# Gate and up projections by seven products of sums of quarters in place of eight, with the sums of the weights formed once

## The chip, the cores and the metric

The kernel runs on one core of one Trainium2 chip. The metric is the device time of one launch in microseconds; the time before is 1982.77 us, the median of 3 runs (1982.16 to 1983.45). All times below that are read from the profile belong to one profiled execution of 1983.66 us, whose span from the first to the last instruction is 1981.9 us.

## The reference

Two layers are applied to x of 2048 tokens by 448 features, each an attention block and then a gated block; the weights are the same in both layers.

```python
def _A_ref(x, wqkv, wo):            # H = 16 heads of 28
    q, k, v = ...                   # x @ wqkv, (1, 16, 2048, 28) each
    scores = jnp.einsum("bhqd,bhkd->bhqk", q, k) * (Dh ** -0.5)
    p = _softmax(scores, axis=-1)
    o = jnp.einsum("bhqk,bhkd->bhqd", p, v)
    return merged(o) @ wo
def _B_ref(x, w_gate, w_up, w_down):
    g = jnp.einsum("bsd,df->bsf", x, w_gate)     # 448 x 1792
    u = jnp.einsum("bsd,df->bsf", x, w_up)       # 448 x 1792
    h = _sigmoid(g) * u
    return jnp.einsum("bsf,fd->bsd", h, w_down)  # 1792 x 448
x = A_x
for _ in range(2):
    x = x + _A_ref(_layernorm(x), A_wqkv, A_wo)
    x = x + _B_ref(_layernorm(x), B_w_gate, B_w_up, B_w_down)
```

All is float32. The kernel gets that accuracy on TensorE by splitting every operand into a high and a low float16 part and adding three products: high by high, high by low, low by high.

## The kernel before

A layer has four stages, one after the other on TensorE: `project` (queries, keys, values), `attend`, `out_project` and `gated`. The order of all work is written out by hand: each engine runs its own instructions in the order of the program, and a semaphore holds an instruction until what it reads is there.

`gated` (L1068) is the stage of the change. Tokens go in four blocks of 512 (`b`), the 1792 hidden features in seven groups of 256 (`p`), so 28 steps in each layer. In a step `by_features_in_fours` (L374) forms four PSUM banks: gate and up for each of two tiles of 128 hidden features, over 512 tokens. The 448 input features are three full slabs of 128 rows and a tail of 64. Each bank takes nine matmuls over the full slabs (L379 to L381), one over the tail with the high part of x in rows 0 to 63 and its low part in rows 64 to 127 (L382, the weights' high part stands in both halves), and one of only 64 rows (L386) for the low part of the tail's weights; these four last ones of 64 rows stand together at the end, two of them in each half of the array's rows. ScalarE then takes the sigmoid (L1125), VectorE multiplies by up (L1126), the product is split in two float16 parts (`split`, L176), and one step later `down` (L1082) adds 24 matmuls of 448 columns (L1089 to L1091) to four PSUM banks that hold the block's output. All split weights of gate and up lie in SBUF during `gated` (`load_gu`, seven tiles of 1 MB).

The next block's x is made ready during the steps, two pieces a step (`Block.steps`, called by `run_fill`): norm, squares (scaling and 32x32 transposes), store and gather through DRAM (which finish the transposition), two empty pieces, and two pieces that split the gathered slabs (`ready`, `part`, L289). For the first block of the stage the same pieces run in `out_project` (L1013), between its 16 token tiles.

The weights are split once, during the attention of layer 0, by `Prepare` (L715): first all tiles are read and measured (for a scale), one every 4 key tiles of attention, then they are read again and split on VectorE (`split`, L804, one every 6 key tiles), and GpSimd's DMA queue carries them to DRAM (`gu_parts`, `write`). A head of attention has 16 key tiles. Two rings of two slots hold the raw tiles and the packed ones.

In `attend` ScalarE takes the exponential of groups of three score tiles (L879). A few tiles are left to VectorE instead (`score_aside`, L881; the table `side`, L850): one in each of heads 0 to 8 of layer 0 and two in each other head. The lines that set it:

```python
        both = 9 if layer == 0 else 0
        for h in range(H):
            for at, kc, qb in ((4, 10, 3), (9, 15, 1)) if h >= both else ((6, 15, 1),):
                side[(h * NT + at) * NB] = (h * NT + kc) * NB + qb
```

SBUF is handed out in slots (`Slots`): 19 of 8 KB per partition (`big`) and 12 of 2 KB (`qrt`), first freed, first used again.

Of the kernel before, what the change touches and what calls it, by code (L numbers as in the profile page):

```python
# [36 lines left out]
XS = 2.0 ** 11  # L37
PS = 2.0 ** -14
# [8 lines left out]
ROUND = 12583039.0  # L47

# [40 lines left out]
def interleaved_layers(ctx: ExitStack, tc: tile.TileContext, x_in, wqkv, wo, w_gate, w_up,  # L89
# [103 lines left out]
    def scaled_low(lo, hi, raw, m):  # L193
        nc.vector.scalar_tensor_tensor(lo, raw, up[:, m:m + 1], hi, op0=ALU.mult,
                                       op1=ALU.subtract)
# [27 lines left out]
    class Block:  # L223


        def __init__(self, b, twice=False):
            self.b = b
            self.twice = twice
# [22 lines left out]
        def parts(self):  # L251
            self.all = big.get("xhl", [P, 8, W], F16)
            self.hi, self.lo = self.all[:, 0:3, :], self.all[:, 3:6, :]
            self.tail = self.all[:, 6, :]
            self.upper = self.all[:, 7, :]
# [26 lines left out]
        def gather(self):  # L282
            rows = self.scr.rearrange("j r i n -> (j r) (i n)")
            self.raw = big.get("xraw", [P, 4, W])
            nc.sync.dma_start(self.raw[:, 0:3, :],
                              rows[0:384].rearrange("(k p) n -> p k n", p=P))
            nc.sync.dma_start(self.raw[0:64, 3, :], rows[384:D])

        def part(self, kt):  # L289
# [7 lines left out]
            else:  # L297
                split_tail(self.tail.rearrange(order, t=TB, i=4), raw)
                if self.twice:
                    nc.scalar.copy(self.upper[64:128].rearrange(order, t=TB, i=4), raw[0:64])  # L300
                big.put(self.raw)

        def steps(self):
            return [self.norm, self.squares,
                    lambda: (self.store((nc.sync, nc.scalar)), self.gather()),
                    lambda: None, lambda: None,
                    lambda: self.ready(0, 1), lambda: self.ready(2, 3)]
# [49 lines left out]
        def drop(self):  # L357
            big.put(self.all)
# [15 lines left out]
    def by_features_in_fours(pms, blk, wh, wl):  # L374


        for o, pm in enumerate(pms):
            for kt in range(3):
                nc.tensor.matmul(pm, wh(o, kt), blk.hi[:, kt, :], start=(kt == 0), stop=False)  # L379
                nc.tensor.matmul(pm, wh(o, kt), blk.lo[:, kt, :], start=False, stop=False)  # L380
                nc.tensor.matmul(pm, wl(o, kt), blk.hi[:, kt, :], start=False, stop=False)  # L381
            nc.tensor.matmul(pm, wh(o, 3), blk.tail, start=False, stop=False)  # L382
        for o, pm in enumerate(pms):
            r = slice(64 * (o % 2), 64 * (o % 2) + 64)
            x = blk.upper if o % 2 else blk.tail
            nc.tensor.matmul(pm, wl(o, 3)[r], x[r], start=False, stop=True,  # L386
                             tile_position=(r.start, 0))
# [16 lines left out]
    gu_parts = dpool.tile([NF // 2, P, 2, 2, 4, 2 * P], F16, name="gu_parts")  # L404
# [310 lines left out]
    class Prepare:  # L715


        def __init__(self):
# [4 lines left out]
            order = [(do, what) for do in (self.measure, self.split) for what in tiles]  # L723
# [3 lines left out]
            for i, (do, what) in enumerate(order):  # L727
# [3 lines left out]
                at += 4 if do == self.measure else 6  # L731
# [14 lines left out]
        def read(self, kind, j):  # L746
# [3 lines left out]
            elif kind == "gu":  # L750
                for i, w in enumerate((w_gate, w_up)):
                    load_rows(self.view(self.next, kind)[:, i], w, j * 2 * P, 2 * P, nc.gpsimd)
            else:
# [8 lines left out]
        def view(self, t, kind):  # L762
            if kind == "gu":
                return t.rearrange("p (w s c) -> p w s c", w=2, s=4)
            return t[:, 0:4 * D].rearrange("p (s n) -> p s n", s=4)

        def step(self, do, what, then):
# [3 lines left out]
            self.write()  # L771
            do(raw, *what)

        def write(self):
            if self.pack:
                nc.gpsimd.dma_start(*self.pack)
                self.pack = None

# [16 lines left out]
        def sizes(self):  # L795
# [5 lines left out]
            nc.vector.tensor_scalar(back[:, 3:4], pw.bitcast(F32)[:, 4:5], 2.0 ** 40, None,  # L801
                                    op0=ALU.mult)

        def split(self, raw, kind, j):  # L804
# [5 lines left out]
            elif kind == "gu":  # L810
                t = big.at(self.packs, "pack", [P, 2, 2, 4, 2 * P], F16)
                for w in range(2):
                    scaled_split(t[:, w, 0], t[:, w, 1], v[:, w], 4 + w, nc.vector)
                self.pack = (gu_parts[j], t)
# [24 lines left out]
    def attend(layer, values, heads, last_values, gate, keep):  # L839
# [11 lines left out]
        both = 9 if layer == 0 else 0  # L851
        for h in range(H):
            for at, kc, qb in ((4, 10, 3), (9, 15, 1)) if h >= both else ((6, 15, 1),):
                side[(h * NT + at) * NB] = (h * NT + kc) * NB + qb
        main = [u for u in range(units) if u not in side.values()]
# [110 lines left out]
        def more(g):  # L966
            if g >= groups:
                return
            for u in main[3 * g:3 * g + 3]:
                if u in side:  # L970
                    begin.append(side[u])
                if u % (NT * NB) == 8:
# [6 lines left out]
                    elif h == H - 1:  # L979
                        gate.load_out()  # L980
                        gate.load_gu()
# [8 lines left out]
        few = both * NT * NB  # L990
        turn = main.index(few) / 3
        paces = (few + both) / max(turn, 1), (quarters + len(side) - few - both) / (groups - turn)
        for g in range(2, groups + 3):
            more(g)
            x = g - 2.25
            due = int(min(x, turn) * paces[0] + max(x - turn, 0) * paces[1])
# [16 lines left out]
    def out_project(outs, gate):  # L1013
# [15 lines left out]

        gate.load_dn()  # L1030
        gate.load_gu()
# [18 lines left out]
    class WeightsGated:  # L1050
        def __init__(self):
            self.gu, self.dn = [], []
# [5 lines left out]
        def load_gu(self):  # L1058
            self.gu.append(big.get("gu", [P, 2, 2, 4, 2 * P], F16))
            nc.sync.dma_start(self.gu[-1], gu_parts[len(self.gu) - 1])  # L1060
# [7 lines left out]
    def gated(layer, first, wt, before_next):  # L1068
        last = layer == LAYERS - 1
        gu, dn = wt.gu, wt.dn  # L1070
        while len(gu) < 7:
            wt.load_gu()
            if 2 * len(dn) < len(gu):
                wt.load_dn()

        seq = [(b, p) for b in range(NB) for p in range(NF // 2)]
# [3 lines left out]
        accs = {}  # L1080

        def down(b, f, hl):  # L1082
            if f == 0:
                accs[b] = [bank(j, "dnp")[:, 0:D] for j in range(TB)]
            dw = dn[f // 4][:, f % 4]
            for j in range(TB):
                s = slice(j * P, (j + 1) * P)
                pm = accs[b][j]
                nc.tensor.matmul(pm, hl[:, 0, s], dw[:, 0, :], start=(f == 0), stop=False)  # L1089
                nc.tensor.matmul(pm, hl[:, 0, s], dw[:, 1, :], start=False, stop=False)  # L1090
                nc.tensor.matmul(pm, hl[:, 1, s], dw[:, 0, :], start=False, stop=(f == NF - 1))  # L1091
                if f == NF - 1:
# [6 lines left out]
            if b == NB - 1 and (f % 4 == 3 or f == NF - 1):  # L1099
                big.put(dn[f // 4])  # L1100

        for b, p in seq:
# [7 lines left out]
            blk = blks[b]  # L1110
            g = gu[p]
            pms = [bank(4 + i, "gate" if i % 2 == 0 else "up") for i in range(4)]

            def part(i):
                return lambda o, kt: g[:, o % 2, i, kt, (o // 2) * P:(o // 2 + 1) * P]

            by_features_in_fours(pms, blk, part(0), part(1))
            if b == NB - 1:
                big.put(g)
            if p == NF // 2 - 1:  # L1120
                blk.drop()
            sigs = [qrt.get("sig", [P, W]) for _ in range(2)]
            hls = [qrt.get("hhl", [P, 2, W], F16) for _ in range(2)]
            for a in range(2):
                nc.scalar.activation(sigs[a], pms[2 * a], AF.Sigmoid, scale=gate_scale)  # L1125
                nc.vector.scalar_tensor_tensor(sigs[a], pms[2 * a + 1], PS, sigs[a],  # L1126
                                               op0=ALU.mult, op1=ALU.mult)
            for a in range(2):
                split(hls[a][:, 0, :], hls[a][:, 1, :], sigs[a])
                qrt.put(sigs[a])  # L1130
            for d in pend:
                down(*d)
            pend = [(b, 2 * p + a, hls[a]) for a in range(2)]
# [82 lines left out]
```

## Time and profile before

| what | before |
|---|---|
| median of 3 runs | 1982.77 us |
| profiled execution, its span | 1983.66 us, 1981.9 us |
| TensorE busy in the span | 1960.6 us |
| ScalarE, VectorE, GpSimd busy | 1162.3, 1069.5, 101.9 us |
| granted TensorE clock, mean | 0.998 |
| `gated`, one step (b, p) | 13.82 us |
| `gated`, first product of layer 0, of layer 1 | at 613.81, at 1589.13 us |

A line of instructions in the profile gives the program line, the engine, the operation, the tile written and the tiles read (buffer numbers left out), the shapes as partitions by elements, the count, and after the bar the busy time in us, the mean in ns of one, and the idle time of the engine just before these instructions. For a matmul the shape "128*128 128x512" is a weight tile of 128 rows by 128 columns and 512 columns that stream through it. PE is TensorE's matmul, PEld its weight load, DVE is VectorE, ACT ScalarE, POOL GpSimd, SP the queue of SyncE. In a timeline the first number is the start in us, the second how long it took; the duration of a matmul includes its way through the array, so the time that a matmul costs in a stream is the distance to the start of the next one. Every matmul of float16 has its own weight load.

### The profile page before, as it was taken

Reading aid. Unit: us, or ns where it says so; the run is one execution under the profiler, and the core shown is the slowest. Engines: PE = TensorE matmul, PEld = TensorE weight load, DVE = VectorE, ACT = ScalarE, POOL = GpSimd, SP = SyncE. Lnnn points to the kernel's source line nnn. Section 1 sums busy time; section 2 is a strip of 40 time slices with the busy share of each in tenths; the row PEclk is TensorE's granted clock in tenths of the full one; section 3 lists DMA queues with packets and bytes.
Section 4 is the critical chain, followed back from the end, with each engine's and each line's share of the span. In section 5 each row is a group of like instructions: output and inputs, shape, how many; then the busy total and the mean of one; then the engine's idle time right before and its main releaser. Section 6 shows DMA issues by size and latency. Waiting matters only on the chain. (4 is left out here: it accounts for less than half of the span.)

```text
span 1981.9 us, 48270 instructions
## 1 busy us (share of the span) xinstructions
PE 1960.6 (99%) x21557; PEld 1009.1 (51%) x21557; DVE 1069.5 (54%) x1661; ACT 1162.3 (59%) x1125; POOL 101.9 (5%) x186
## 2 busy tenths in 40 slices
PE   9999999999999999999999999999999999999999
PEld 4445555555554444444444555555565544444444
DVE  6647888677765232323265487677766632323222
ACT  5559999999961212121145799999999312121111
POOL 2013323000000000000000000000000000000000
PEclk9999999999999999999999999999999999999999
DMA  5565668211025101010243311111111250101000
GB/s 168 159 194 163 178 190 266 67 48 49 19 76 197 38 1 38 8 30 12 82 123 128 91 45 49 32 48 49 45 35 47 73 204 1 56 1 56 1 19 19
DMA packets 84842, 153.78 MB, mean 78 GB/s; under 512 B 9584, under 2 KB 60368, under 8 KB 81808
## 3 DMA queue, kind: packets, MB, share of 16 engines
q1 hardware_dynamic: 67488, 111.80, 18.3%
q0 software_dynamic: 8448, 34.41, 5.7%
q10 hardware_dynamic: 8688, 4.36, 0.9%
q8 instruction: 173, 2.83, 0.6%
q14 instruction: 45, 0.37, 0.1%
HBM read 97.52 MB, written 45.68 MB: 72 GB/s over the span
## 5 line engine op out<-in xcount | busy, mean ns | idle before, releaser
L879 ACT ACTIVATE prob_s<-sc 128x1536 f32<-128x1536 f32 x665 | 893.2, 1532 | 4.9 <-DMA qp_s<-qk_scr 3.6
L915 PE MATMUL acc<-prob_s,val_s 128*32 128x384 f32 (+3 forms) x7904 | 567.0, 381 | 0.0
L864 PE MATMUL sc<-qp_s 114*32 114x512 f16 x7972 | 555.6, 380 | 3.9 <-issue 1.7
L1125 ACT ACTIVATE sig_q<-gate 128x512 f32<-128x512 f32 x112 | 60.8, 594 | 597.4 <-PE up L386 597.4
L864 PEld LDWEIGHTS <-qp_s 114*32 114x32 f16 x8192 | 253.2, 95 | 227.8 <-issue 111.2
L1126 DVE SCALAR_TENSOR_TENSOR sig_q<-up,sig_q 128x512 f32<-128x512 f32 x112 | 72.2, 686 | 513.9 <-ACT sig_q L1125 513.9
L915 PEld LDWEIGHTS acc<-prob_s,val_s 128*32 128x32 f32 x7904 | 264.8, 110 | 156.3 <-issue 12.9
L1089 PE MATMUL dnp<-dn_s,hhl_q 128*128 128x448 f16 x448 | 158.4, 354 | 0.0
L1090 PE MATMUL dnp<-dn_s,hhl_q 128*128 128x448 f16 x448 | 157.9, 352 | 0.0
L1091 PE MATMUL dnp<-dn_s,hhl_q 128*128 128x448 f16 x448 | 157.9, 352 | 0.0
L372 PE MATMUL qkp<-xhl_s,wqk_s 128*128 128x512 f16 x616 | 139.6, 379 | 1.8 <-DVE xhl_s L184 0.7
L379 PE MATMUL gate<-xhl_s,gu_s 128*128 128x512 f16 x336 | 127.3, 379 | 3.0 <-ACT xhl_s L178 2.1
L380 PE MATMUL gate<-xhl_s,gu_s 128*128 128x512 f16 x336 | 127.3, 379 | 1.4 <-DVE xhl_s L179 1.4
L381 PE MATMUL up<-xhl_s,gu_s 128*128 128x512 f16 x336 | 127.3, 379 | 0.0
L379 PE MATMUL up<-xhl_s,gu_s 128*128 128x512 f16 x336 | 127.3, 379 | 0.0
L380 PE MATMUL up<-xhl_s,gu_s 128*128 128x512 f16 x336 | 127.3, 379 | 0.0
L381 PE MATMUL gate<-xhl_s,gu_s 128*128 128x512 f16 x336 | 127.3, 379 | 0.0
L941 DVE COPY oraw_q<-acc 128x512 f32<-128x512 f32 x32 | 22.1, 692 | 179.5 <-PE acc L915 179.4
L895 DVE SCALAR_TENSOR_TENSOR power_q<-power_q,expo_q 128x512 f32<-128x512 f32 x165 | 114.2, 692 | 5.6
L943 DVE RECIPROCAL oden_q<-oden_q 128x512 f32<-128x512 f32 x32 | 107.3, 3353 | 1.1
L381 PEld LDWEIGHTS <-gu_s 128*128 128x128 f16 x672 | 65.7, 98 | 81.3 <-issue 2.5
L380 PEld LDWEIGHTS <-gu_s 128*128 128x128 f16 x672 | 65.7, 98 | 80.9 <-issue 3.5
(152 smaller groups left out, 2012.7 us busy)
## 6 DMA issues: line engine op xcount, KB each, us to landing
qp_s<-qk_scr SPq DMA_DIRECT2D x96, 224.0 KB
qk_scr<-qkhl_q SPq DMA_DIRECT2D x56, 256.0 KB
gu_s<-gu_parts SPq DMA_DIRECT2D x14, 1024.0 KB
xraw_s<-xt_scr SPq DMA_DIRECT2D x14, 768.0 KB
xt_scr<-xs_s SPq DMA_DIRECT2D x38, 224.0 KB
qp_s<-qk_scr SPq DMA_DIRECT2D x64, 112.0 KB
gu_parts<-pack_s POOLq DMA_DIRECT2D x7, 1024.0 KB, 7.5
raw_s<-in_B_w_down_dram POOLq DMA_DIRECT2D x6, 896.0 KB, 8.4
```

The source lines that it names most:

```text
L372: nc.tensor.matmul(pm, w, x, start=(i == 0), stop=(i == len(terms) - 1))
L379: nc.tensor.matmul(pm, wh(o, kt), blk.hi[:, kt, :], start=(kt == 0), stop=False)
L380: nc.tensor.matmul(pm, wh(o, kt), blk.lo[:, kt, :], start=False, stop=False)
L381: nc.tensor.matmul(pm, wl(o, kt), blk.hi[:, kt, :], start=False, stop=False)
L864: nc.tensor.matmul(ps[32 * j:32 * j + 32, :], hd.k[:, keys], hd.q[:, qb * W:(qb + 1) * W], start=True, stop=True, tile_position=(0, 32 * j))
L879: nc.scalar.activation(prob[:, 0:n, :], ps[:, 0:n, :], AF.Exp, scale=exp_scale)
L895: nc.vector.scalar_tensor_tensor(p, p, c[k], y, op0=ALU.add, op1=ALU.mult)
L915: nc.tensor.matmul(acc[qb * VC:(qb + 1) * VC, s], v[:, kc % TB, h, :], probs[c * NB + qb][:, s], start=(kc == 0 and a == 0), stop=(kc == N ...
L943: nc.vector.reciprocal(den, den)
L1089: nc.tensor.matmul(pm, hl[:, 0, s], dw[:, 0, :], start=(f == 0), stop=False)
L1090: nc.tensor.matmul(pm, hl[:, 0, s], dw[:, 1, :], start=False, stop=False)
L1091: nc.tensor.matmul(pm, hl[:, 1, s], dw[:, 0, :], start=False, stop=(f == NF - 1))
```

## The change

With the input features cut in two halves (rows 0 to 255 and 256 to 447, filled up with zeros to 512), the hidden features in two halves of 896 and the tokens of a block in two of 256, each of gate and up is a 2 by 2 product of quarters, of which seven products with sums of quarters on both sides suffice. A step p now takes the tile of 128 hidden features p and the tile p + 7.

- `gate_and_up` replaces the four banks. For each of gate and up, `of_halves` issues seven products with 256 columns of x: four of them of six matmuls (`k < 4`), three of five matmuls (`k >= 4`), of which the fourth takes the tail of 128 rows (the low part of the weights stands under the high part, and the high part of x in both halves) and the fifth only rows 0 to 63. The partial sums are kept by going on in the same PSUM bank; ScalarE copies six states of it, VectorE adds them.
- `half_steps` replaces the two pieces `ready`: seven pieces that form four differences of x and split seven operands.
- `Prepare` forms four sums of the weights on GpSimd for each of 14 tiles (`add_up`), and splits ten operands, one tile every 5 key tiles of attention.
- `WeightsGated`: a step's weights are two tiles of 800 KB. Three of the seven pairs stay in SBUF; those of steps 1, 2, 4 and 5 share two places and are read again by GpSimd's queue (`used`).
- In layer 0, the tiles left to VectorE are 19 in place of 23 (`FEW`).

```diff
+AFTER = (None, 4, 5, None, 1, 2, None)
+N_SUMS = 25
+SHORT = ((10, 23, 12), (11, 24, 13), (8, 22, 9))
+FEW = "1111010101"
...
+            def subtract(name, a, b):
+                t = qrt.get(name, [P, 2, W // 2])
+                a, b = [v if len(v.shape) == 5 else ordered(v) for v in (a, b)]
+                for k in range(2):
+                    nc.vector.tensor_tensor(ordered(t)[:, k], a[:, k], b[:, k],
+                                            op=ALU.subtract)
+                return t
...
+            def r11():
+                self.wide = big.get("xwide", [P, 4, 2, 2, W // 2], F16)
+                self.short = big.get("xshort", [P, 3, 2, 2, W // 2], F16)
+                self.t1 = subtract("t1", cut(0, 2), cut(0, 0))
+                divide(self.wide[:, 0], cut(0, 0))
...
+            return [r11, t1, t2, t3, r21, t4, r22]
...
-            nc.tensor.matmul(pm, wh(o, 3), blk.tail, start=False, stop=False)
-        for o, pm in enumerate(pms):
-            r = slice(64 * (o % 2), 64 * (o % 2) + 64)
-            x = blk.upper if o % 2 else blk.tail
-            nc.tensor.matmul(pm, wl(o, 3)[r], x[r], start=False, stop=True,
-                             tile_position=(r.start, 0))
+    def of_halves(pm, w, blk, k, first):
+        if k < 4:
+            x = blk.wide[:, k]
+            terms = [(w[:, i], x[:, j, t]) for t in range(2)
+                     for i, j in ((2 * k + t, 0), (2 * k + t, 1), (14 + 2 * k + t, 0))]
+        else:
+            x = blk.short[:, k - 4]
+            main, low, tail = SHORT[k - 4]
+            terms = [(w[:, main], x[:, 0, 0]), (w[:, main], x[:, 1, 0]), (w[:, low], x[:, 0, 0]),
+                     (w[:, tail], x[:, 0, 1]), (w[0:64, tail], x[0:64, 1, 1])]
+        for i, (a, x) in enumerate(terms):
+            nc.tensor.matmul(pm, a, x, start=(first and i == 0),
+                             stop=(i == len(terms) - 1), skip_group_check=True)
...
-                at += 4 if do == self.measure else 6
+                at += 4 if do == self.measure else 5
...
+        def add_up(self, v):
+            s12, s34 = [qrt.get("sums", [P, 2, 2, P]) for _ in range(2)]
+            l11, l12, l21, l22 = v[:, 0:2, 0], v[:, 2:4, 0], v[:, 0:2, 1], v[:, 2:4, 1]
+            for to, a, b, op in ((s12[:, 0], l21, l22, ALU.add),
+                                 (s12[:, 1], s12[:, 0], l11, ALU.subtract),
+                                 (s34[:, 0], l11, l21, ALU.subtract),
+                                 (s34[:, 1], l12, s12[:, 1], ALU.subtract)):
+                nc.gpsimd.tensor_tensor(to, a, b, op=op)
+            return s12, s34
...
+        def used(self, b, p):
+            after = AFTER[p]
+            if b == NB - 1 and (after is None or after < p):
+                big.put(*self.gu.pop(p))
+            elif after is not None:
+                big.put(*self.gu.pop(p))
+                self.load_gu(after, nc.gpsimd)
...
+            def on_chain(m, k, to):
+                pm = chain[m][:, lo]
+                of_halves(pm, w[m], blk, k, k == 0)
+                nc.scalar.copy(to, pm)
...
+            first(0)
+            first(1)
+            apart(0)
+            second(0)
+            second(1)
+            apart(1)
+            third(0)
+            third(1)
+            c11_c22(0)
+            c11_c22(1)
+            sigmoid(one[0], one[0])
+            c21(0)
+            sigmoid(two[0][:, hi], chain[0][:, lo])
+            c21(1)
+            times(one[0], one[1])
+            times(two[0][:, hi], chain[1][:, lo])
+            c12(0)
+            sigmoid(two[0][:, lo], two[0][:, lo])
+            c12(1)
+            times(two[0][:, lo], two[1][:, lo])
```

`first`, `second`, `third` and `apart` are the products of six matmuls (k = 0, 2, 3 and 1); `c11_c22`, `c21` and `c12` are those of five (k = 4, 5 and 6), and m is 0 for gate and 1 for up. `cut(k, t)` is a quarter of the gathered x, `divide` splits it: two copies on ScalarE and two subtractions on VectorE for a quarter of x, one of each over 512 columns for a difference. In `out_project` two pairs of weight tiles are now loaded ahead of the first block's store and gather, where it was one tile of 1 MB.

243 lines of the change are left out of this document (171 added, 72 removed).

## The prediction

> **What bounds the kernel now.** I read the page's totals first, then the busy times by stage, then the order of instructions in one step of `gated`, and last the rows of the engines that the change loads.
>
> ```profile
> PE 1960.6 (99%) x21557; PEld 1009.1 (51%) x21557; DVE 1069.5 (54%) x1661; ACT 1162.3 (59%) x1125; POOL 101.9 (5%) x186
> ...
> 260.00:360.00 100.00, 100.00 (x1820) 57.58 (x1816) 80.71 (x94) 99.90 (x75) 30.73 (x51) 1.00 0.68 214
> ...
> 800.00:900.00 100.00, 100.00 (x496) 45.75 (x495) 32.60 (x56) 20.96 (x37) 1.20 (x2) 1.00 0.07 19
> ```
>
> The columns of the last two lines are the window, then the busy time of PE, PEld, DVE, ACT and POOL, the granted clock, the DMA share and GB/s. In `gated` (800 to 900) TensorE alone is full, at full clock, VectorE works a third of the time, ScalarE a fifth. So a step there costs what its matmuls cost in a stream, and copies, additions and weight traffic are free as long as they stay beside it. In the attention of layer 0 (260 to 360) TensorE and ScalarE are both full and VectorE works 81%: that stage has little room. What a matmul costs is the distance between starts:
>
> ```profile
> 798.90 0.38 PE L381 MATMUL up<-xhl_s,gu_s 128*128 128x512 f16 x1
> 798.90 0.10 PEld L382 LDWEIGHTS <-gu_s 128*128 128x128 f16 x1
> 799.12 0.38 PE L382 MATMUL up<-xhl_s,gu_s 128*128 128x512 f16 x1
> 799.42 0.11 PEld L386 LDWEIGHTS <-gu_s 64*128 64x128 f16 x4 [0.42 <-issue]
> 799.43 0.39 PE L386 MATMUL gate<-xhl_s,gu_s 64*128 64x512 f16 x1
> 799.43 0.39 PE L386 MATMUL up<-xhl_s,gu_s 64*128 64x512 f16 x1
> 799.65 0.38 PE L386 MATMUL gate<-xhl_s,gu_s 64*128 64x512 f16 x1
> 799.66 0.38 PE L386 MATMUL up<-xhl_s,gu_s 64*128 64x512 f16 x1
> 799.96 0.10 PEld L1089 LDWEIGHTS <-hhl_q 128*128 128x128 f16 x1 [0.42 <-issue]
> 799.97 0.36 PE L1089 MATMUL dnp<-dn_s,hhl_q 128*128 128x448 f16 x1
> ...
> 804.52 0.38 PE L379 MATMUL gate<-xhl_s,gu_s 128*128 128x512 f16 x1
> ...
> 1087.76 0.27 PE L515 MATMUL qnorm<-sq_q,ind 128*128 128x256 bf16 x1
> 1087.87 0.27 PE L518 MATMUL knorm<-sq_q,ind 128*128 128x256 bf16 x1
> 1087.97 2.54 PE L372 MATMUL qkp<-xhl_s,wqk_s 128*128 128x512 f16 x11
> ```
>
> Between two matmuls of the same weight tile (128 by 128) the load starts with the matmul before it and is hidden: 799.12 - 798.90 = 0.22 us for 512 columns (ten of them from 804.52 take 2.15, so 0.2155). Where the tile goes from 128 rows to 64 (799.12 to 799.43) or back (799.66 to 799.97), the load waits until the running matmul has streamed out, and the distance is 0.31: 0.095 more, a whole load (0.10 to 0.11). The two 64-row pairs run two at a time, so a step pays this twice only. Matmuls of 256 columns with full weight tiles follow at 0.11, half of 0.2155 and a nanosecond: 0.109, and the next load (0.10) still fits.
>
> **The matmuls of a step.** The step is 13.82 us long (799.97 against 786.15 a step before). Its `down` part is 24 matmuls from 799.97 to 804.52, 4.55 us; so gate and up take 9.27 (42 times 0.2155 is 9.05, two changes of tile 0.19). Afterwards each of gate and up has 4 products of 6 and 3 of 5 matmuls, 39 of 256 columns, 78 in all: 78 x 0.109 = 8.50. That alone would be 0.77 less. But six of the 78, the fifth of each `k >= 4` product, have 64 rows, and each stands alone between full tiles: the four before it, and after it the next product or `down`. That is 6 ways in and 6 ways out, 12 x 0.094 = 1.13. Sum 9.63, so +0.36 a step, and with 56 steps **+20 us**. Bounds: no exposed load, -43 us (rival one); a full 0.11 for each of 12 and 0.11 for each matmul, 9.90, +35 us. I take 0.094 since both directions are in the trace at that size, and also another partial tile at the array's corner, followed by a full one:
>
> ```profile
> 1098.81 0.35 PE L394 MATMUL vp<-wv_s,xhl_s 128*128 128x448 f16 x1
> ...
> 1099.09 0.20 PE L665 MATMUL bounds<-ident,bnd 16*1 16x16 f32 x2
> ...
> 1099.22 0.36 PE L396 MATMUL vp<-wv_s,xhl_s 128*128 128x448 f16 x1
> ```
>
> (448 columns cost 0.19, the distance is 0.28; the way back costs 0.10 beyond the 16 columns.)
>
> The Trainium skill (TensorE: Matmul & The Clock Gate, Part 2, step 1) says that a weight load is pulled ahead of running matmuls where the row groups don't conflict or where it goes to the background weight buffer. For full tile after full tile the trace agrees (0.22 with the load inside); read as holding for 64 rows too it gives the -43 us, and against that stands the 0.31 at 799.12.
>
> **What stays beside the matmuls in a step.** ScalarE: six copies of 256 columns, sigmoids of 512 and twice 256, two splits of 512. The rows give 594 ns (L1125) and 618 ns (L178) for 512; for 256 I take 0.38: 6 x 0.38 + 0.6 + 0.76 + 1.24 = 4.9 us of 14.2. VectorE: about ten operations of 0.4 to 0.69, 5 us. No bank is written again before another product or two has passed (`second(0)` starts two products, 1.3 us, after `first(0)` ends; the last matmul's way out, 0.38 - 0.2155, and the copy need 0.55), so I cost these at nothing; without that cover each late copy would cost its own 0.4 us, twelve of them a step. The pieces for the next block's x add some 2 us of VectorE and 1 us of ScalarE each, twice a step; VectorE is next needed 5.9 us into the next step and ScalarE 0.65, both behind the 4.55 of `down`: nothing. The reloads (two of 800 KB) are queued on POOL behind the end of a step's gate and up and are needed two steps, 28 us, later; 1024 KB of POOL's took 7.5 us to land. Queued behind them on POOL is the next block's `norm`; VectorE waits for it at the most some 2 us in a place with 5 to spare. Nothing.
>
> **The start of `gated`, twice.** Now:
>
> ```profile
> 613.14 1.66 ACT L178 CAST xhl_s<-xraw_s 128x512 f16<-128x512 f32 x3 [21.25 <-DMA xraw_s<-xt_scr]
> 613.81 0.38 PE L379 MATMUL gate<-xhl_s,gu_s 128*128 128x512 f16 x1 [1.09 <-ACT xhl_s L178]
> 614.53 0.38 PE L380 MATMUL gate<-xhl_s,gu_s 128*128 128x512 f16 x1 [0.35 <-DVE xhl_s L179]
> ```
>
> TensorE already waits for the gathered x and its splits, about 2 us in all. Afterwards VectorE must do a difference (0.8) and a split (0.7 to 0.8) for each of the first four operands, with `out_project`'s last additions (0.68 each) between them in its order: about 2.3 us for each, where TensorE needs 0.65 to 1.3. Going through that order, the fourth operand is there 8.3 us after the gather and TensorE has waited 4.7 by then. That is +2.7; 2.3 MB more weights ahead of the store on SP's queue may add up to 1 us (the queue's load is done by about 601, when the store starts). Twice: **+6 us**, bounds 0 and 15.
>
> **Attention of layer 0.** Four tiles go from VectorE to ScalarE, which is full: 75 groups of three in 100 us is 1.33 us a group, 4/3 of it is **+2 us**. `Prepare` now has 14 tiles of split in place of 7. On VectorE one is ten operations; with L189's rows (1024 elements 748 ns, 1792 1149) and L194's (1284, 2084) that is 1.8 + 3.2 = 5.0 us every 5 key tiles, where it was 4.1 every 6. A head is 28 us (16 key tiles of 1.75): a head with one tile aside then asks 16 (splits) + 6.2 (aside) + 6.6 (end of head) + 1.8 (memset) = 30.6 of VectorE, one without 24.4; they alternate, so it just fits.
>
> GpSimd is the doubt. For each of the 14 it issues four reads (0.78 and 0.53, twice: 2.6 us), waits for the last to land (5 to 6 us after its issue), then does four two-input operations of 256 elements that no row shows. The nearest rows:
>
> ```profile
> L244 POOL TENSOR_TENSOR rs<-rs,nhalf 128x4 f32<-128x4 f32 x14 | 14.2, 1012 | 1.2
> ...
> L499 POOL MEMSET val_s<- 128x256 f32 x8 | 2.7, 341 | 4.7 <-DVE xs_s L265 3.3 <-PE up L386 1.5
> ```
>
> I take 0.6 (nearer to the memset, which has the same length; L244 is a power): 7.3 + 2.4 = 9.7 us a tile, against 5 x 1.75 = 8.75 of pace. VectorE's next split waits for that sum, and behind it stand the exponentials aside and the copy at the end of a head (L941) that frees a PSUM bank; TensorE waits when they are over some 10 us late. Lag 14 x 0.95 = 13, less one tile of lead: 4 us. I take **+4 us**; bounds 0 (at 0.34 it keeps pace) and 25 (at 1.01 a tile takes 11.4, lag 37 less 12 of slack).
>
> For the price of such an addition the Trainium skill (GPSIMD Engine Reference, section 3.1) has 4497 ns for 2048 elements, an estimate of 0.56 for 256, by which the lag would be 11 and the cost some 3 us; no trace here shows it.
>
> **Sum.** 1983.66 (the profiled execution) + 20 + 6 + 2 + 4 = 2015.7. It stands 0.9 above the median of the runs, so about 2015; I say 2015.
>
> **Rivals.** One, on the other side: the load of a lone 64-row tile hides, as that of a full tile does. Place: the fifth matmul of each short product; then a step is 8.50 + 4.55 and 56 of them save 43: 1983 - 43 + 12 = 1952. It decides once fewer than about 5 of the 12 loads are exposed. For it: the upper half of the rows is idle. Against: 0.31 each way above, and the corner tile at 1099. Chance 0.07.
>
> Two, GpSimd's additions are slow and hold VectorE, ScalarE and TensorE in layer 0's attention: 25 in place of 4, 2036. For it: four tiles' worth of VectorE slack at the most, and the shared stage is full. Against: the tiles aside are few there. Chance 0.14.
>
> Three, reloads or copies come late in each step: one microsecond in each of 28 reloads, or half a microsecond in each of 56 steps, is 28: 2043. Against: 28 us for two landings of 7.5, and a third of each engine used. Chance 0.05.
>
> Four, small costs at the bottom of all bounds and half the exposure: within 0.2% of before. Chance 0.02.
>
> **Chances and range.** The forecast has the rest, 0.72, with its own range of 2003 to 2030. The whole range is 1997 to 2042: it leaves out rival one and most of three. A measurement here tells about 0.2%, 4 us, from no change: faster 0.07, same 0.02, slower 0.91.
>
> **What would show it.** A step of `gated` of about 14.2 us, with distances of 0.11 between full tiles and 0.20 on both sides of each 64-row matmul; no idle time of TensorE named for ScalarE or VectorE inside a step; first product of `gated` with some 5 us of waits around it; in layer 0 GpSimd's additions and what VectorE waits for before its splits. Steps of 13.1 us would make the prediction wrong, as would GpSimd additions over 1 us.

## The result and the profile after

| | before | after |
|---|---|---|
| median of 4 runs each | 1983.11 us (1982.16 to 1984.02) | 2047.95 us (2045.44 to 2050.78) |
| profiled execution, its span | 1983.66, 1981.9 us | 2045.44, 2043.7 us |
| granted TensorE clock, mean | 0.998 | 0.991 |

The changed kernel takes 1.0327 times as long (95% interval 1.031 to 1.0345), about 65 us more. The forecast was 2015 (+32) with 2003 to 2030 for the likeliest case and 1997 to 2042 in all: the direction and the largest term were right, the size was half of what came. Of the eight runs of the first experiment below one took 4106.59 us, over twice the other seven, for a reason that no trace shows; its figures there are of the seven.

The spans of the two profiled executions differ by 61.8 us. Cut at the first matmul of each stage, they divide like this:

| stage on TensorE | before, us | after, us | more | forecast |
|---|---|---|---|---|
| up to the first matmul of `project` | 14.3 | 15.7 | 1.4 | 0 |
| `project`, layer 0 and 1 | 213.9 | 215.0 | 1.1 | 0 |
| `attend`, layer 0 | 455.7 | 465.5 | 9.9 | 6 |
| `attend`, layer 1 | 447.6 | 448.1 | 0.6 | 0 |
| `out_project`, layer 0 and 1 | 69.0 | 70.7 | 1.7 | 0 |
| `gated`, layer 0 and 1 | 781.5 | 828.7 | 47.2 | 26 |

The 47.2 of `gated` have two parts. A step, from the first `down` matmul to the next step's, is 14.310 us where it was 13.817: 0.493 more, 56 times, 27.6 (forecast 20). The rest, 9.9 in layer 0 and 9.7 in layer 1, comes once in each stage, at its start: 19.6 (forecast 6). The step is steady: all 52 that can be measured inside a layer take 14.31.

The page's totals after, and the busy times of the two windows that the prediction showed (PE, PEld, DVE, ACT, POOL, then granted clock, DMA share, GB/s):

```profile
PE 1994.4 (98%) x23405; PEld 1183.3 (58%) x23405; DVE 1267.8 (62%) x2125; ACT 1324.3 (65%) x1582; POOL 201.8 (10%) x341
...
260.00:360.00 100.00, 92.97 (x1628) 49.70 (x1623) 82.75 (x123) 90.77 (x69) 63.69 (x96) 0.95 0.51 165
...
800.00:900.00 100.00, 100.00 (x715) 66.17 (x714) 51.81 (x102) 38.74 (x90) 6.10 (x11) 1.00 0.26 85
```

In `gated` (800 to 900) TensorE is still the only full engine and at full clock: VectorE went from 33 to 52 us, ScalarE from 21 to 39, and neither reaches TensorE. In the attention of layer 0 (260 to 360) TensorE lost 7 us and some clock, ScalarE lost 9.

The stream of a step after, on TensorE; a line with x6, x10 or x12 holds several matmuls and shows the shape of the first (the x10 holds two 64-row ones too), and what they cost is the distance to the next line's start:

```profile
848.44 1.47 PE L480 MATMUL chain<-xwide_s,gu_s 128*128 128x256 f16 x12
849.75 0.82 PE L480 MATMUL side<-xwide_s,gu_s 128*128 128x256 f16 x6
850.40 1.47 PE L480 MATMUL chain<-xwide_s,gu_s 128*128 128x256 f16 x12
851.71 0.82 PE L480 MATMUL side<-xwide_s,gu_s 128*128 128x256 f16 x6
852.37 1.47 PE L480 MATMUL chain<-xwide_s,gu_s 128*128 128x256 f16 x12
853.68 1.57 PE L480 MATMUL side<-xshort_s,gu_s 128*128 128x256 f16 x10
855.18 1.04 PE L480 MATMUL chain<-xshort_s,gu_s 128*128 128x256 f16 x6
```

Twelve matmuls of the products with full tiles take 849.75 - 848.44 = 1.31, 0.109 each, as forecast. Ten of two products with a 64-row tile take 855.18 - 853.68 = 1.50, where ten at 0.109 would take 1.09: each of the two lone 64-row tiles costs 0.20 more. Over all steps the median distance is 0.205 on the way into such a tile and 0.212 on the way out, so 0.096 and 0.103 above the 0.109; the matmul after that one follows at 0.12, another 0.01. That is 0.21 for a tile, 0.105 for each change.

The reloads land early: they take 5.0 us and are needed two steps, 28 us, later.

```profile
gu_s<-gu_parts POOLq DMA_DIRECT2D x56, 800.0 KB, 5.0
```

The start of `gated` in layer 0, on ScalarE and TensorE; what stands in brackets is the idle time before the line and what ended it:

```profile
626.65 0.27 PE L480 MATMUL chain<-xwide_s,gu_s 128*128 128x256 f16 x1 [2.16 <-ACT xwide_s L353]
...
627.27 1.37 PE L480 MATMUL chain<-xwide_s,gu_s 128*128 128x256 f16 x11 [0.35 <-DVE xwide_s L354]
...
629.47 0.71 PE L480 MATMUL side<-xwide_s,gu_s 128*128 128x256 f16 x5 [0.72 <-DVE xwide_s L358]
...
633.85 0.40 ACT L361 COPY xshort_s<-xshort_s 64x256 f16<-64x256 f16 x1 [1.91 <-DVE xshort_s L354]
...
637.28 0.40 ACT L361 COPY xshort_s<-xshort_s 64x256 f16<-64x256 f16 x1 [0.52 <-DVE xshort_s L354]
637.71 0.65 ACT L1278 COPY one_q<-chain 128x256 f32<-128x256 f32 x2
638.13 2.72 PE L480 MATMUL chain<-xwide_s,gu_s 128*128 128x256 f16 x12 [7.96 <-ACT one_q L1278]
640.65 1.48 PE L480 MATMUL side<-xwide_s,gu_s 128*128 128x256 f16 x6
```

TensorE waits 7.96 us for a copy of a PSUM bank by ScalarE (L1278). The product that it copies ended before 630; the copy is 0.65 us for two. But it stands on ScalarE behind the pieces t3, r21, t4 and r22 of the block's x, which `out_project` issues (the last three of them all at its end, by `run_fill(steps, 9)`), and each of those waits for VectorE (1.91 us ahead of 633.85, and so on). TensorE needs nothing of what these pieces make until some 4 us later: `third(0)` at 641.93 is the first to read t3's operand, and the other three are first read at 643.51. The twelve matmuls from 638.13 take 2.52 us in place of 1.31, and the granted clock says why (window, busy times, clock):

```profile
628.00:632.20 4.20, 1.45 (x12) 1.00 (x11) 4.20 (x11) 1.85 (x4) 0.00 (x0) 1.00 1.02 418
632.30:638.00 5.70, 0.00 (x0) 0.00 (x0) 2.97 (x7) 2.82 (x8) 0.00 (x0) 0.50 1.02 417
638.00:642.40 4.40, 4.26 (x21) 2.94 (x21) 0.00 (x0) 1.10 (x4) 0.00 (x0) 0.50 1.01 412
642.50:652.00 9.50, 9.50 (x77) 6.79 (x76) 5.07 (x9) 4.59 (x11) 0.00 (x0) 1.00 0.04 15
```

The clock falls to 0.50 during the wait, some 2 us after TensorE stopped, and stays there until 642.4, 4.3 us after the restart. Half of these 4.3 us is lost, and that much is missing: 1.2 over the first twelve matmuls, 0.9 over the next eighteen. Together with the waits behind the stage's first matmul, 0.35 + 0.72 + 7.96 = 9.03 where the two largest had been 0.35 and 0.34, that makes up the 9.9 to within half a microsecond.

In the attention of layer 0 one place stands out, the end of a head. On TensorE and ScalarE:

```profile
335.84 0.83 PE L999 MATMUL sc<-qp_s 114*32 114x512 f16 x12
...
343.70 0.62 PE L999 MATMUL aside<-qp_s 114*32 114x512 f16 x4 [7.03 <-DVE oraw_q L1076]
...
344.94 1.52 PE L999 MATMUL sc<-qp_s 114*32 114x512 f16 x12
...
346.57 1.45 ACT L1014 ACTIVATE prob_s<-sc 128x1536 f32<-128x1536 f32 x1 [8.09 <-PE sc L999]
```

And on VectorE up to the copy that TensorE waits for:

```profile
335.40 0.60 DVE L203 TENSOR_SCALAR pack_s<-raw_s,up 128x256 f16<-128x256 f32 x1 [2.94 <-DMA gu_parts<-pack_s]
...
338.26 1.27 DVE L208 SCALAR_TENSOR_TENSOR pack_s<-sums_q,up,pack_s 128x512 f16<-128x512 f32 x2
...
341.16 1.76 DVE L561 MEMSET qp_s<- 18x2048 f16 x1 [0.48 <-issue]
342.96 0.69 DVE L1076 COPY oraw_q<-acc 128x512 f32<-128x512 f32 x1
```

A score tile left to VectorE (`aside`) takes a PSUM bank that holds the previous head's `acc` until VectorE has copied it. VectorE gets to that copy (342.96) after the splits of a weight tile (L203, L208), which had themselves waited 2.94 us for the write of an earlier packed tile, and the memset. So TensorE stops, and ScalarE after it. The groups that follow start at 344.94 and 347.50, 2.56 us apart in place of 1.35, at a granted clock of 0.50, which lasts until 348.9. So this late copy costs its wait and 2.6 us more, half of the 5.2 us of low clock behind it. The waits of this kind sum to 7.8 us in this execution.

### The profile page after: what moved, and what is told of

Its sections match the earlier page's. It is cut to its first block, busy times and chain, and to the rows that moved or that the text cites. A ratio compares the mean times of both kernels' runs of the same rounds, so it can differ in the third digit from the quotient of the medians.

```text
span 2043.7 us, 53439 instructions
## 1 busy us (share of the span) xinstructions
PE 1994.4 (98%) x23405; PEld 1183.3 (58%) x23405; DVE 1267.8 (62%) x2125; ACT 1324.3 (65%) x1582; POOL 201.8 (10%) x341
## 5 line engine op out<-in xcount | busy, mean ns | idle before, releaser
L1050 PE MATMUL acc<-prob_s,val_s 128*32 128x128 f32 (+3 forms) x7870 | 567.8, 383 | 0.0
L480 PEld LDWEIGHTS <-gu_s 128*128 128x128 f16 (+1 forms) x4368 | 404.2, 98 | 177.6 <-issue 93.7
L1294 DVE TENSOR_TENSOR one_q<-side,one_q 128x512 f32<-128x512 f32 x112 | 76.6, 688 | 327.6 <-PE side L480 324.5
L480 PE MATMUL chain<-xwide_s,gu_s 128*128 128x256 f16 x2016 | 250.6, 274 | 20.1 <-ACT one_q L1278 15.9
L1278 ACT COPY one_q<-chain 128x256 f32<-128x256 f32 x224 | 82.9, 372 | 218.9 <-PE chain L480 218.8
L480 PE MATMUL side<-xshort_s,gu_s 128*128 128x256 f16 (+1 forms) x1120 | 176.1, 276 | 0.0
L465 PEld LDWEIGHTS <-wqk_s 128*128 128x128 f16 x616 | 60.1, 98 | 72.0 <-issue 4.5
L480 PE MATMUL side<-xwide_s,gu_s 128*128 128x256 f16 x672 | 93.2, 275 | 1.4 <-DVE xwide_s L358 1.4
L480 PE MATMUL chain<-xshort_s,gu_s 128*128 128x256 f16 (+1 forms) x560 | 88.3, 276 | 0.0
L1278 ACT COPY two_q<-chain 128x256 f32<-128x256 f32 x112 | 41.7, 372 | 70.2 <-PE chain L480 70.2
```

The lines of the kernel that those rows point to most:

```text
L465: nc.tensor.matmul(pm, w, x, start=(i == 0), stop=(i == len(terms) - 1))
L480: nc.tensor.matmul(pm, a, x, start=(first and i == 0), stop=(i == len(terms) - 1), skip_group_check=True)
L1050: nc.tensor.matmul(acc[qb * VC:(qb + 1) * VC, s], v[:, kc % TB, h, :], probs[c * NB + qb][:, s], start=(kc == 0 and a == 0), stop=(kc == N ...
L1278: nc.scalar.copy(to, pm)
L1294: nc.vector.tensor_tensor(one[m], side[m], one[m], op=ALU.add)
```

## The experiments

**The 64-row tiles.** The fifth matmul of the short products takes all 128 rows of its weight tile. In two of the three short products the rows added are zero in x; in the third they add a low part times a low part, which is next to nothing. The number of matmuls is the same and only the tile's shape differs.

```diff
-                     (w[:, tail], x[:, 0, 1]), (w[0:64, tail], x[0:64, 1, 1])]
+                     (w[:, tail], x[:, 0, 1]), (w[:, tail], x[:, 1, 1])]
```

> The fifth matmul of each short product takes all 128 rows of its weight tile and of x in place of 64; the upper rows then meet the low part of x, which is zero there for two of the three products and adds a low part by a low part (2^-22 of the size) for the third. Theory A (each change between a 64-row and a 128-row weight tile exposes one weight load): all distances in gate and up become 0.11, 12 times 0.1 us fall away, the step goes from 14.31 to 13.1 us, 56 steps save 68: about 1980. Rival B (the step is longer because 78 matmuls of 256 columns, or the copies between them, cost more than their columns): the step stays above 14 us and the time above 2030.

Measured: 1980.17 us (1976.97 to 1985.16, seven runs) against 1982.33 for the kernel before, ratio 0.999 (0.9977 to 1.0003); a step is 13.055 us (in 7 steps 13.22). The place that took 1.50 us for ten matmuls:

```profile
856.08 1.25 PE L480 MATMUL side<-xshort_s,gu_s 128*128 128x256 f16 x10
...
857.17 1.04 PE L480 MATMUL chain<-xshort_s,gu_s 128*128 128x256 f16 x8
```

It takes 1.09. So the twelve ways in and out of six lone 64-row tiles cost 14.310 - 13.055 = 1.255 us a step, 0.105 each, and by the two ratios (1.0327 and 0.999 of 1982) this line of the program alone is worth 67 us, as much as the whole change lost. That the time is then only even with before, though a step is 0.76 shorter than before's (43 us for 56), is because the other two terms stay: a wait of 7.96 us is there at each of the two starts, and the attention of layer 0 is 473.5 us in this execution.

**The same exposure in the old step.** The kernel before, with its 64-row matmul put right behind its bank's tail, so that the four are single and not two pairs:

```diff
             nc.tensor.matmul(pm, wh(o, 3), blk.tail, start=False, stop=False)
-        for o, pm in enumerate(pms):
             r = slice(64 * (o % 2), 64 * (o % 2) + 64)
```

> The kernel before with each of the four 64-row matmuls moved to stand right behind its bank's tail matmul, alone between full tiles, where they stood together in two pairs. Theory A (a lone 64-row tile exposes a load on the way in and on the way out): 8 exposed loads in place of 2 and four single matmuls in place of two pairs, 6 x 0.095 + 2 x 0.2155 = 1.0 us a step, 14.82, 56 steps: about 2039. Rival B (the load of a lone tile hides, only the four loads that come together don't): 0.43 - 0.19 a step, 14.06, about 1996.

Measured: 2041.54 us in one run, a step of 14.873 us.

```profile
804.57 0.38 PE L382 MATMUL gate<-xhl_s,gu_s 128*128 128x512 f16 x1
804.88 0.39 PE L385 MATMUL gate<-xhl_s,gu_s 64*128 64x512 f16 x1
805.20 0.39 PE L379 MATMUL up<-xhl_s,gu_s 128*128 128x512 f16 x1
805.43 0.38 PE L380 MATMUL up<-xhl_s,gu_s 128*128 128x512 f16 x1
```

0.31 into the 64-row tile, 0.32 out of it, 0.23 and less between full ones. The step grew by 1.056: two more matmuls' worth of streaming, since the pairs no longer run two at a time (2 x 0.2155 = 0.431), and six more changes of tile, 0.625 or 0.104 each. The exposure belongs to the change of tile, not to the new products.

**The copies behind the pieces.** The last three pieces of the first block's x (r21, t4, r22) are issued in `gated`, behind copies of its first step, in place of all at the end of `out_project`.

```diff
-        run_fill(steps, 9)
+        first.rest = steps
...
+            rest = blk.__dict__.pop("rest", ())
...
+            run_fill(rest)
```

(`run_fill(rest)` stands behind `second(1)`, `third(0)` and `third(1)`.)

> The last three pieces of the first block's x (r21, t4, r22) are issued inside the first step of gated, after ScalarE's copies second(1) and around third, and not ahead of the whole stage. Theory A (the 8 us of waiting early in each gated are ScalarE's copy of the first product, queued behind these pieces): the wait before the second product on the chain falls from 8 to about 1 us, the waits around the start of the stage from 11.7 to about 4, twice: some 15 us less, about 2033. Rival B (VectorE's differences and splits pace the start, wherever ScalarE's copies stand): at most 2 to 3 us less in each layer, 2043.

Measured: 2038.14 us, ratio 1.0277 (1.0247 to 1.0307). The wait at the same place:

```profile
637.95 2.72 PE L480 MATMUL chain<-xwide_s,gu_s 128*128 128x256 f16 x12 [0.96 <-ACT one_q L1279]
```

7.96 has become 0.96 (in layer 1, 1.48). `gated` went from 412.4 to 406.7 and from 416.4 to 409.8 us; above what the steps explain, 4.2 and 3.2 are left of 9.9 and 9.7. So 12 us of the change's time are the order of the work. The pieces moved on VectorE as well as on ScalarE; that ScalarE's place is the one that counts is read from the trace above. The launch gained less, some 9 to 10 us, as the attention of layer 0 took 473.5 us in the profiled execution here. What is left at the start is the wait for the copy (0.96 and 1.48), one of 0.8 to 0.9 us for VectorE in each layer, and in layer 0 a clock of 0.50 from 634.7 to 641.5.

**GpSimd's additions left out.** `add_up` returns the raw quarters; the sums of the weights are not formed, so gate and up are computed with other weights.

```diff
...
-                nc.gpsimd.tensor_tensor(to, a, b, op=op)
-            return s12, s34
+            return v[:, :, 0], v[:, :, 1]
```

> GpSimd's four additions for each weight tile are left out, and VectorE splits quarters of the raw weights in their place, with as many instructions and elements (so gate and up get other weights). Theory A (GpSimd's sums, 3.3 us a tile, make the splits late, and their traffic slows VectorE): the wait of 7 to 8 us for the copy at the end of a head goes, the attention of layer 0 falls from 465.5 to about 458, the total to 2040. Rival B (VectorE's own 14 splits, five microseconds each, are what is late): the attention of layer 0 stays above 463.

Measured: 2044.13 us, ratio 1.0308 (1.0278 to 1.0337), and the attention of layer 0 takes 466.4 us: no clear gain, as the two intervals overlap. A wait of 6.2 us at the same end of a head is still there:

```profile
PE aside L992 <- DVE oraw_q L1069: 6.2, 1, 6.2
```

(What waits, for what: us in total, times, longest.) The theory that GpSimd's additions set the lag falls. With them out, VectorE waits for other things of the same rings: the write of a packed tile (11.4 us) and the read of a raw one (6.4).

**No tile aside while weights are split.** The heads 4 to 9 of layer 0 leave no tile to VectorE.

```diff
-FEW = "1111010101"
+FEW = "1111000000"
```

> The changed kernel with no tile left to VectorE in heads 4 to 9 of layer 0 (16 tiles aside in that layer in place of 19), one string changed. Theory A (TensorE's waits of 6 to 8 us there are the score tile for VectorE, which needs the PSUM bank that VectorE's late copy at the end of the head before holds): without such a tile no wait over 1 us is left in the attention of layer 0, it takes 455.7 + 7/3 x 1.33 = 459, and the total falls from 2046 by 6 to 14. Rival B (VectorE's lateness reaches TensorE by the output banks or the slots as well): a wait of several microseconds stays, the stage stays above 463.

Measured: 2035.02 us, ratio 1.0269 (1.0249 to 1.029). The attention of layer 0 is 455.97 us, as before the change (455.66), and TensorE has no wait over 1 us left in it:

```profile
260.00:360.00 100.00, 100.00 (x1792) 53.11 (x1791) 73.83 (x123) 100.00 (x75) 66.13 (x101) 1.00 0.55 169
```

GpSimd's work and the splits are all still there, three more tiles went to ScalarE, and the term is gone. But VectorE has less to do without these tiles, so it might just be late no more. How late it is can be measured: from the end of a head's last `acc` product (found by counting the columns of these products) to the start of the copy of `acc`. At the end of head 6, counted from 0:

| run | copy late by, us | TensorE's wait for the tile aside of head 7, us |
|---|---|---|
| before | 0.1 | none |
| after | 12.4 | 7.0 |
| additions left out | 11.5 | 6.2 |
| short splits (below) | 8.7 | 3.4 |
| write first (below) | 18.7 | 13.4 |
| no tile aside (this experiment) | 6.5 | none |
| all three mended (below), no tile aside | 11.6 | none |

Where it waits, the wait is the lateness less 5.3 us. Without one VectorE is still late, in the last row almost as late as in the changed kernel, and TensorE doesn't wait. So what lags on VectorE reaches TensorE only through the tile aside.

**What makes VectorE late.** Two kernels change the load on it. In the first, the low parts of the split gate and up weights are left out: six operations a tile become two plain scalings.

```diff
-                for to, hi, a in ((t[:, 14:16], t[:, 0:2], v[:, 0:2, 0]),
...
-                    scaled_low(to, hi, a, 4 + m)
...
+                for to, a in ((t[:, 14:22].rearrange("p (k z) n -> p k z n", k=4), v),
+                              (t[:, 22:25], s34[:, 0:3])):
+                    scaled_high(to, a, 4 + m, nc.vector)
```

> In layer 0, VectorE's six operations that form the low parts of a weight tile are replaced by two scalings (1.2 us in place of 3.2; the low parts of gate and up are left out, other numbers stand in their places). GpSimd's sums, the reads and the writes stay. Theory A (VectorE's own volume in a head with a tile aside, 30.6 us where 28 are there, is what makes it late): 3.2 splits a head save 6 us, the waits of 7 us for the copy at the end of a head go, the attention of layer 0 is 458 or less. Rival B (VectorE is late because each split waits for a transfer, a packed tile's write or a raw tile's read): the waits for transfers grow by what the splits save, and a wait of TensorE over 4 us stays.

Measured: 2038.42 us, ratio 1.0283 (1.0253 to 1.0314); the attention of layer 0 is 461.0 us and the wait at the end of a head 3.4 us where it was 7.0. Half of the wait goes with VectorE's volume. The other half does not, and the shorter splits mostly move VectorE into another wait, which was 10.9 us in the changed kernel over the same stretch (255 to 420 us):

```profile
DVE pack_s L203 <- DMA gu_parts<-pack_s: 27.0, 4, 9.2
```

In the second, a step of `Prepare` issues the write of a finished tile ahead of the reads of the next:

```diff
         def step(self, do, what, then):
             raw = self.next
+            self.write()
             if then:
                 self.read(*then)
-            self.write()
```

> The changed kernel with GpSimd's order in a step of the preparation turned: the packed tile before is written out first, the next raw tile is read after it. Theory A (volume): nothing changes, the attention of layer 0 stays between 465 and 474. Rival B (a split waits for the write of the tile two before it): the write starts some 3 us sooner, VectorE's waits for transfers fall by as much at each split, and the wait of 7 us for the copy falls to 4 or less.

Measured: 2059.09 us, ratio 1.0388 (1.0358 to 1.0418), the wrong way; the attention of layer 0 is 480.7 us. Now TensorE waits 13.4 and 6.8 us at two heads, and VectorE waits for the sums:

```profile
PE aside L999 <- DVE oraw_q L1076: 20.2, 2, 13.4
...
DVE pack_s L203 <- POOL sums_q L897: 18.4, 10, 4.6
```

The likely reading is that reads that start later make everything behind them later: read, landing, sums, split and write are one round, and VectorE's splits stand in it with no slack. It is not settled how the wait of 7 us divides between VectorE's volume, GpSimd's part of the round and the transfers; the identical code of this stage took 465.5, 473.5 and 473.5 us in three executions (the changed kernel and the experiments on the tiles and on the pieces). The difference is a second wait, at the end of head 8, of 4.3 and 5.7 us where the changed kernel has 0.8. Shown is that the sums alone are not it, that less volume halves it, and that without a tile aside the lateness costs nothing.

**All three mended.** Full rows, later pieces, no tile aside.

> All 128 rows in the fifth matmul, the last three pieces of the first block inside the first step, and no tile aside in heads 4 to 9 of layer 0, together. If the three causes are separate, the gains add: step 13.06, gated 372 and 376 us, attention of layer 0 459, all told about 1957, 1.3% less than the kernel before. If they hide one another (VectorE later at the start of gated when the matmuls are shorter), 1965 or more.

Measured: 1958.31 us (1957.29 to 1959.08) against 1981.43, ratio 0.9882 (0.9865 to 0.9898): 23 us faster than the kernel before, with seven products. The page's totals, and the window in `gated`:

```profile
PE 1927.3 (99%) x23413; PEld 1211.3 (62%) x23413; DVE 1227.2 (63%) x2095; ACT 1317.9 (67%) x1583; POOL 200.0 (10%) x341
...
800.00:900.00 100.00, 100.00 (x782) 76.35 (x781) 51.74 (x106) 42.18 (x102) 6.10 (x11) 1.00 0.28 94
```

782 matmuls in 100 us of `gated` in place of 715, the same clock: that is the exposed loads' time. A step is 13.055 us; `gated` is 16.2 and 15.3 us shorter than before the change, where 28 steps of 0.76 less would give 21.3: the other 5 to 6 us are waits of about 1 us each that remain at the start, the clock after them, and seven steps of 13.2 to 13.5 us.

## Why the prediction was right and wrong

**The matmuls of a step: right in kind, 0.011 us short each.** The number of matmuls, 0.109 between full tiles and twelve exposed loads are what the trace shows. The load was taken as 0.094 from two rounded starts; it measured 0.105 (the first experiment), so the step grew by 0.49 and not 0.36: 27.6 in place of 20. The trace of before had a better value: its step is 13.817, `down` takes 4.55 and 42 matmuls of 0.2155 take 9.05, which leaves 0.217 for two changes of tile, 0.108 each. The prediction wrote 9.27 beside 9.05 + 0.19 and let the 0.03 between them go, which is 0.014 for each of two changes; the new step has twelve.

**Rival one fell.** It had the lone 64-row tile's load hidden, and the upper half of the rows idle for it. 0.205 and 0.212 on the two sides of each such tile, and 1.255 us a step won by filling its rows up, show that it isn't. The Trainium skill (TensorE: Matmul & The Clock Gate, Part 2, step 1) says that a load is pulled ahead of running matmuls where the row groups don't conflict or the background buffer takes it. This trace shows the load hidden from full tile to full tile (0.109) and not across a change of the tile's size (0.205 and 0.212).

**What stays beside the matmuls: right in the steady step.** TensorE is 100% busy in the window from 800 to 900 with VectorE at 52% and ScalarE at 39%, and rival three (late reloads and copies in each step) fell with the landing time of 5.0 us.

**The start of `gated`: the step that failed.** Forecast 6 (0 to 15), measured 19.6, outside its bounds. The prediction went through VectorE's order only, by when the operands of the first four products are there, and that part was about right (waits of 0.35 and 0.72). The copies of PSUM by ScalarE were costed at nothing, with the cover of a steady step: two products between `first(0)` and `second(0)`. At the start of a stage that cover doesn't hold, since ScalarE has the stage's own preparation ahead of the copy in its order, and that preparation waits for VectorE. Before, the stage had no such copies: ScalarE's first work on a bank was the sigmoid, behind a whole step's gate and up. The experiment on the pieces took away 12 of the 19.6. About 2 of each start, the low clock around the restart, was in no term.

**Attention of layer 0: the place and the +2 right, the cause of the +4 not.** Forecast 6, measured 9.9 (and up to 18 in other executions). The 9.9 hides something: the stage's first head varies between executions, 37.7 us before, 35.6 in the kernel with single 64-row tiles, whose code there is the same, and 35.5 after. From its end to the end of the stage it is 417.98 in both of the first two and 430.0 after, 12.0 more. In the two kernels without tiles aside while weights are split, where seven tiles moved to ScalarE and nothing waits, it is 420.9, so 0.41 for each tile: the four tiles cost 1.7, as the +2 said. With 7.8 of waits and 2.6 of low clock that is the 12.0. So the +4 measured 10.4.

The prediction named the wait: the end of a head's copy that frees a bank, behind the splits, in a stage whose VectorE "just fits". It let the lag be 13 us, with some 10 us late as the point from which TensorE waits. The copy came 12.4 late, but by another cause, so that agreement is luck; and the wait begins at 5.3, half of the slack that was counted on. It put the lag on GpSimd's additions at 0.6 us. They measured more, 0.75 to 0.85:

```profile
L897 POOL TENSOR_TENSOR sums_q<-raw_s 128x256 f32<-128x256 f32 x28 | 23.8, 851 | 29.8 <-DMA raw_s<-in_B_w_up_dram 13.3 <-DMA raw_s<-in_B_w_gate_dram 9.6 <-issue 7.0
```

but without them the wait stayed, so rival two, GpSimd as the cause with 25 us, fell too. What does make the copy late stays open, as said above. (The estimate of 0.56 that was worked out from the Trainium skill, GPSIMD Engine Reference, section 3.1, for this size is low: the measured value is a third to a half above it.)

**The sum.** 27.6 + 19.6 + 9.9 = 57.1 of 61.8; the other 4.7 are in stages that the prediction costed at nothing, 1.4 ahead of the first matmul of `project`, 1.7 in `out_project` (of it the longer wait for the first operands, 2.16 in place of 1.09), 1.1 in `project`, 0.6 in the second attention; no experiment took these apart. The median of the changed kernel is 2.5 us above its profiled execution.

## What to carry to other kernels

Keep the weight tiles of a stream the same size: a lone tile of 64 rows between tiles of 128 saves nothing and costs two weight loads, and filling its rows up was worth 67 us here; take the price of such a thing from the length of a whole repeating step rather than from two starts. Where a stage begins, go through the order of every engine, not only of the one that makes the operands: a short copy that frees or saves a bank may stand behind preparation that nobody needs yet. And a bank that is shared with late work (here a tile aside that waits for the last head's copy) couples an engine with little slack to the one that is the bound; without that tie the same lag of 12 us cost nothing here.

## What the runs showed of the hardware that was not expected

- A change of the weight tile from 128 to 64 rows or back costs a whole load at both sizes of matmul: 0.096 in and 0.103 out at 256 columns (and 0.01 more at the matmul after), 0.104 on average at 512.
- TensorE's granted clock fell to 0.50 while it was still waiting, 1.5 to 2 us into the waits of 7 and 8 us, and stayed there until 5.2 us (attention) and 4.3 us (`gated`, layer 0) after the restart, then 1.00. Half of that time was lost, 2.6 and 2.1 us. In the changed kernel's trace each of these stretches lasted 10.2 us. A shorter wait can cost something too: in the kernel with all three mended one of 2.3 us, at the start of `gated`, was followed by 3.4 us at 0.50.
- VectorE slows down beside GpSimd's additions: scaling 512 elements a row to float16 took 713 ns with them (first line, the changed kernel, 255 to 395 us) and 488 ns in the kernel that leaves them out (second fence, same window). It shows within the changed kernel's trace as well: two such operations took 1.90 us from 322.50, while GpSimd added, and 1.01 us from 328.32, while it issued transfers.

```profile
L203 DVE TENSOR_SCALAR pack_s<-sums_q,up 128x512 f16<-128x512 f32 x24 | 16.1, 713 | 0.0
```

```profile
L203 DVE TENSOR_SCALAR pack_s<-raw_s,up 128x512 f16<-128x512 f32 x39 | 16.8, 488 | 0.0
```
